# Prologue of a fused attention and maxout kernel: E and F turned together, keys of batch 0 projected four heads at once, fp32 filler

## The chip, the core and the metric

The kernel runs on one core of one Trainium2 chip. The metric is the device time of one execution in microseconds, the median of several runs. The profile shows one further execution; its span goes from the first to the last instruction, and its own time is a little longer than its span.

## What is computed

Linformer attention over 8 batches, 8 heads, 1024 positions and a head dimension of 64, followed by a maxout layer:

```python
k_proj = einsum('ks,bhsd->bhkd', E, k)            # E, F: 64 x 1024
v_proj = einsum('ks,bhsd->bhkd', F, v)
attn   = softmax(q @ k_proj^T / 8)                # over the 64 projected keys
x      = (attn @ v_proj), heads side by side      # 8192 x 512
h      = maximum(maximum(x @ w1, x @ w2), x @ w3) # 512 -> 768
out    = h @ w_out                                # 8192 x 512, float32
```

All inputs are float32 in memory. The kernel computes in bf16 with float32 accumulation.

## The kernel before

The work goes batch by batch, each batch in two halves of 512 positions. For every half the three maxout products (l1, L216), and the product with w_out (L240) fill TensorE; the attention of the next batch is put between them at slots written out by hand. The order of the instructions on every engine is the order of the program: the kernel has a manual schedule, and an engine that waits holds what stands behind it.

**The prologue** (L363 to L506) does batch 0 before that machinery runs, since nothing is loaded yet. It works on the first half of batch 0 (ch 0), with heads in pairs (groups g = 0 to 3; HEAD gives the order of heads 0, 1, 2, 3, 5, 4, 7, 6), while loads arrive.

*Loads.* SyncE and ScalarE issue E, F and the first half of q as float32 (L366 to L370). POOL issues all loads that change the type from float32 to bf16, in one queue: four of k (two heads each), three of v, the first of four parts of w1, the last of v, the other parts of w1, then w2, w3, the second half of q, w_out and the data of batch 1 (L378 to L393, L477 to L481). Eight of these may be under way; each later one waits for the one eight before it.

*E and F.* Each is held as 128 rows of 512 (two rows of the tile to a row of E), cast to bf16 (E on VectorE L401, F on ScalarE L402), and turned by multiplying with the identity, 16 matmuls of 64 columns each (L406), into one PSUM bank each. E is copied out on VectorE, F on ScalarE (L413). Before it copies F, ScalarE casts two pairs of q (L412). fT2 holds F twice side by side (L451), for wide value projections.

*Queries.* Cast by head (L423, L424), turned on TensorE in groups of two heads (q_turn0, L417), copied out on VectorE (L419).

*Keys.* k_proj0(g) (L275) projects one pair of heads: 16 matmuls with the keys as stationary operand, 64 columns each, which gives the projected keys already turned, heads on partitions. A cast (L280) puts them into kpT.

*Values.* v_proj0(g) (L282) does the same for the groups 0 and 1; v_wide0(g) (L289) does the groups 2 and 3 with the doubled F, 8 matmuls of 128 columns, and two copies.

*Scores and softmax.* scores0 (L298) and exp0 (L304) per group, into the banks SB = (0, 1, 4, 5). sums_part0(hh) (L312) sums over keys by multiplying with ones, for the head half hh (groups 0 and 1, or 2 and 3), and takes logarithm and inverse on ScalarE. kp_up0 (L325) spreads the projected keys by a selection matrix for the scores of the second half of the batch, used much later; VectorE copies them out (L330).

*Attention output and w1.* av0(f, hh) (L474) multiplies with the values; norm0 (L318) scales on VectorE and writes xT. w1_ct(ct) (L456) adds part ct of w1 for all six column tiles jt, each in its own bank W1B = (0, 1, 4, 5, 2, 3). The parts ct 0 and 1 need head half 0, the parts 2 and 3 head half 1. From w1_ct(1) on TensorE goes on with w2 and w3 (l1_first, L461).

The order on TensorE from the first half of the sums on is: the exponentials of all four groups are issued, sums_part0(0), v_proj0(0), kp_up0, sums_part0(1), fillers, v_proj0(1), a filler, av0 for head half 0, v_wide0(2), a filler, w1_ct(0), v_wide0(3), half of w1_ct(1), av0 for head half 1, and the rest of w1.

*Fillers.* warmup(n, bank) (L359) runs n matmuls of 512 columns on a tile of zeros whose result is not used. 24 of them stand in the prologue.

Of the kernel before, what the change touches and what calls it, by code (L numbers as in the profile page):

```python
# [9 lines left out]
FP32 = mybir.dt.float32  # L10
# [6 lines left out]
def kernel(ctx: ExitStack, tc: tile.TileContext, q, k, v, E, F, w1, w2, w3, w_out, out):  # L17
# [25 lines left out]
    eT = T([P, SI, KP], BF16, "eT")  # L43
    fT2 = T([P, SI, 2, KP], BF16, "fT2")
    fT = fT2[:, :, 0, :]
# [25 lines left out]
    ef_f = ef_b.bitcast(FP32).rearrange("p (x n) -> p x n", n=S // 2)  # L71
    ef_b = ef_b[:, 2 * S:3 * S].rearrange("p (x n) -> p x n", x=2)
# [45 lines left out]
    AB = 4  # L118
# [156 lines left out]
    def k_proj0(g):  # L275
        for si in range(SI):
            for u in range(2):
                nc.tensor.matmul(out=ps[u * D:(u + 1) * D, 2, g * KP:(g + 1) * KP], lhsT=k_t[0][:, HEAD[2 * g + u], si, :],
                                 rhs=eT[:, si, :], start=(si == 0), stop=(si == SI - 1))
        nc.vector.tensor_copy(out=kpT[0][:, g, 0, :], in_=ps[:, 2, g * KP:(g + 1) * KP])  # L280

    def v_proj0(g, bank):  # L282
        for si in range(SI):
            for u in range(2):
                nc.tensor.matmul(out=ps[half(g, u), bank, g * D:(g + 1) * D], lhsT=fT[:, si, :],
                                 rhs=v_t[0][:, HEAD[2 * g + u], si, :], start=(si == 0), stop=(si == SI - 1))
        nc.vector.tensor_copy(out=vp2[0][:, g], in_=ps[:, bank, g * D:(g + 1) * D].rearrange("p (dd f) -> p f dd", f=2))
# [10 lines left out]
    def scores0(ch, g, bank):  # L298
        for u in range(2):
            rows = slice(u * D, (u + 1) * D)  # L300
            nc.tensor.matmul(out=ps[half(g, u), bank, :], lhsT=kpT[0][rows, g, 0, :],
                             rhs=qT[0][rows, 4 * ch + g, :], start=True, stop=True)
# [9 lines left out]
    def sums_part0(hh):  # L312
        cols = slice(hh * 512, (hh + 1) * 512)
        quads0(0, 6, lambda rows, g: ones[rows, :], (hh,))
        nc.scalar.activation(out=lns[0][:, cols], in_=ps[:, 6 + hh, :], func=AF.Ln)
        nc.scalar.activation(out=rinv[0][:, cols], in_=lns[0][:, cols], func=AF.Exp, scale=-1.0)
# [8 lines left out]
    def kp_up0():  # L325
        for u in range(2):
            for f in range(2):
                nc.tensor.matmul(out=ps[:, u, f * 256:(f + 1) * 256], lhsT=sel[:, 2 * u + f, :],
                                 rhs=kpT[0][:, 0:NPAIR, 0, :], start=True, stop=True)
            nc.vector.tensor_copy(out=kp_0[:, u].rearrange("p f g k -> p (f g k)"), in_=ps[:, u, :])  # L330
# [7 lines left out]
    def scores_up0():  # L338
        for g in range(NPAIR):
            for f in range(2):  # L340
                for r in range(4):
                    rows = slice(r * HD, (r + 1) * HD)
                    for u in range(2):
                        nc.tensor.matmul(out=ps[half(g, u), AB + r, g * P:(g + 1) * P], lhsT=kp_0[rows, u, f, g, :],  # L344
                                         rhs=qT_1[rows, HEAD[2 * g + u]].rearrange("p (n f) -> p n f", f=2)[:, :, f],
                                         start=(f == 0), stop=(f == 1), tile_position=(r * HD, half(g, u).start))
# [15 lines left out]


    nc.scalar.preload_act_table_set("natural_log_exp_and_others")
    nc.vector.memset(warm, 0.0)
    nc.sync.dma_start(out=ef_f[:, 0], in_=E.rearrange("k (x n) -> (k x) n", x=2))  # L366
    nc.scalar.dma_start(out=ef_f[:, 1], in_=F.rearrange("k (x n) -> (k x) n", x=2))
# [32 lines left out]
    warmup(9, 7)  # L400
    nc.vector.tensor_copy(out=ef_b[:, 0], in_=ef_f[:, 0])  # L401
    nc.scalar.copy(out=ef_b[:, 1], in_=ef_f[:, 1])  # L402
    for y, dst in enumerate((eT, fT)):
        for si in range(SI):
            for x in range(2):
                nc.tensor.matmul(out=ps[x * D:(x + 1) * D, y, si * KP:(si + 1) * KP], lhsT=ef_b[:, y, si::SI],  # L406
                                 rhs=ident[:, x::2], start=True, stop=True)
        if not y:
            warmup(2, 3)
        if y:  # L410
            for g in (0, 1):
                nc.scalar.copy(out=q_0[:, :, 2 * g, :], in_=q_st[:, HEAD[2 * g]])  # L412
        (nc.scalar.copy if y else nc.vector.tensor_copy)(out=dst, in_=ps[:, y, :].rearrange("p (si k) -> p si k", k=KP))  # L413
# [7 lines left out]
    def q_cast0(g):  # L421
        if g > 1:
            nc.scalar.copy(out=q_0[:, :, 2 * g, :], in_=q_st[:, HEAD[2 * g]])  # L423
        nc.vector.tensor_copy(out=q_0[:, :, 2 * g + 1, :], in_=q_st[:, HEAD[2 * g + 1]])  # L424
# [7 lines left out]
    k_proj0(0)  # L432
    q_turn0(2)
    warmup(1, 3)
    k_proj0(1)
    scores0(0, 0, SB[0])
    exp0(0, 0, SB[0])
    q_turn0(3)
    warmup(1, 3)
    k_proj0(2)  # L440
    scores0(0, 1, SB[1])
    exp0(0, 1, SB[1])
    warmup(2, 3)
    k_proj0(3)
    scores0(0, 2, SB[2])
    exp0(0, 2, SB[2])
    warmup(1, 3)
    scores0(0, 3, SB[3])
    exp0(0, 3, SB[3])
    sums_part0(0)  # L450
    nc.vector.tensor_copy(out=fT2[:, :, 1, :], in_=fT)  # L451
# [30 lines left out]
    v_proj0(0, 3)  # L482
    kp_up0()
    sums_part0(1)
    warmup(3, 2)
    v_proj0(1, 3)
    warmup(1, 2)
# [4 lines left out]
    v_wide0(2, 3)  # L492
    warmup(1, 2)
# [145 lines left out]
```

## Time and profile before

| what | value |
|---|---|
| median of 3 runs | 395.08 us (394.8 to 395.1) |
| profiled execution, its own time | 394.77 us |
| its span | 392.9 us |
| granted TensorE clock, mean | 1.000 |
| instructions in the span | 6611 |
| first matmul of w1 (L458) | starts 18.26 us |
| first matmul of w2 and w3 (L467) | starts 25.03 us |
| first matmul of the steady stage (L216) | starts 42.83 us |

How to read the profile: PE is TensorE, PEld its weight loads, DVE VectorE, ACT ScalarE, POOL GpSimd, SP SyncE. Times are in microseconds from the first instruction of the span. In a timeline each row is a run of like instructions: start, length, engine, line, operation, out<-in, shape, count, and in brackets how long the engine had been idle ahead of it and what released it. In the chain that ended last each row is a start, a length and what the time went to. A few matmul records are missing from a trace, so counts can be a little low.

### The profile page before, as it was taken

What the parts mean: (1) busy time and instruction counts of PE and PEld (TensorE: products, weight loads), DVE (VectorE), ACT (ScalarE), POOL (GpSimd) and SP (SyncE); (2) the same over time, 40 slices, a digit from 0 to 9 for tenths busy, and PEclk for the clock granted to TensorE, in tenths of its full rate; (3) what the DMA queues carried; (4) which work ended last, traced back from release to release, by engine and by line L of the source; (5) the groups of instructions that cost most, each with busy time, mean ns of one, the idle gap of its engine ahead of it and who ended that gap; (6) DMA issues with size and microseconds to landing.
All of it is one profiled execution on the core that took longest, in us unless ns stands there. A gap on an engine that the chain in (4) does not pass through costs nothing.

```text
span 392.9 us, 6611 instructions
## 1 busy us (share of the span) xinstructions
PE 383.7 (98%) x2695; PEld 172.8 (44%) x2746; DVE 202.9 (52%) x305; ACT 162.2 (41%) x248; POOL 67.0 (17%) x110
## 2 busy tenths in 40 slices
PE   8999999999999999999999999999999999999996
PEld 4444444444444444444444444444444444444443
DVE  4447475755662566344753357524764446453341
ACT  4413448374326622454224732266134542222222
POOL 7452131072004300050000600000010000000000
PEclk9999999999999999999999999999999999999999
DMA  8999979799984994169511992131011111111022
GB/s 224 206 211 204 205 184 199 125 209 206 206 159 89 200 206 177 26 123 204 158 53 28 176 212 97 53 81 54 2 60 48 54 55 54 55 46 60 5 104 107
DMA packets 41309, 48.39 MB, mean 123 GB/s; under 512 B 9152, under 2 KB 36288, under 8 KB 41280
## 3 DMA queue, kind: packets, MB, share of 16 engines
q0 software_dynamic: 31792, 43.52, 54.1%
q1 hardware_dynamic: 8656, 3.54, 4.7%
q10 hardware_dynamic: 832, 0.92, 0.7%
q8 instruction: 21, 0.34, 0.3%
q14 instruction: 8, 0.07, 0.1%
HBM read 57.15 MB, written 16.78 MB: 188 GB/s over the span
## 4 chain that ended last, share of the span: by engine, by line
PE 93%; DMA 5%; issue 1%; ACT 1%; POOL 0%; POOLq 0%
PE ps L216 60%; PE ps L240 19%; PE ps L124 3%; PE ps L160 3%; DMA w_sb<-in_moe_w_dram 3%; PE ps L467 2%; PE ps L146 2%; DMA k_t<-in_k_dram 2%; PE ps L254 1%; PE ps L458 1%; ACT pT L348 1%; PE ps L272 0%; PE ps L233 0%; POOL k_t L376 0%; PE ps L344 0%
## 5 line engine op out<-in xcount | busy, mean ns | idle before, releaser
L216 PE MATMUL ps<-xT,w_sb 128*128 128x512 bf16 x1048 | 242.6, 379 | 1.7
L216 PEld LDWEIGHTS <-w_sb 128*128 128x128 bf16 x1080 | 103.7, 98 | 129.8 <-issue 8.0
L221 DVE TENSOR_TENSOR m<-ps,h1s 128x512 f32<-128x512 f32 x90 | 62.1, 690 | 131.1 <-PE ps L216 100.6
L240 PE MATMUL ps<-wo_sb,hT 128*128 128x512 bf16 x342 | 84.0, 379 | 0.4
L219 ACT COPY h1s<-ps 128x512 f32<-128x512 f32 x90 | 52.9, 588 | 72.7 <-PE ps L216 72.0
L242 ACT COPY o_acc<-ps 128x512 f32<-128x512 f32 x59 | 34.6, 586 | 100.6 <-PE ps L240 86.0
L223 DVE TENSOR_TENSOR hT<-ps,m 128x512 bf16<-128x512 f32 x90 | 62.0, 689 | 8.1
L247 POOL DMA_DIRECT2D out_dram<-o_acc x28 | 15.2, 542 | 252.4 <-ACT o_acc L242 245.9
L240 PEld LDWEIGHTS <-hT 128*128 128x128 bf16 x354 | 34.0, 98 | 42.2 <-issue 2.3
L180 DVE TENSOR_TENSOR xT<-ps,rinv 128x1024 bf16<-128x1024 f32 x28 | 33.4, 1218 | 11.3 <-PE ps L160 11.3
L151 ACT ACTIVATE pT<-ps 128x1024 bf16<-128x1024 f32 x28 | 27.1, 1020 | 4.8 <-PE ps L146 4.4
L106 DVE STREAM_TRANSPOSE qT<-q_t 128x512 f32<-128x512 f32 x28 | 18.5, 689 | 0.0
L90 POOL DMA_DIRECT2D v_t<-in_v_dram x21 | 15.3, 754 | 9.4 <-issue 3.5
L171 ACT ACTIVATE lns<-ps 128x1024 f32<-128x1024 f32 x14 | 13.6, 1023 | 3.9 <-PE ps L160 3.9
L174 ACT ACTIVATE rinv<-lns 128x1024 f32<-128x1024 f32 x14 | 14.8, 1061 | 0.0
L124 PE MATMUL ps<-k_t,eT 128*64 128x512 bf16 x56 | 13.4, 382 | 0.0
L126 PE MATMUL ps<-v_t,fT 128*64 128x512 bf16 x56 | 13.4, 382 | 0.0
L90 POOL DMA_DIRECT2D k_t<-in_k_dram x14 | 10.7, 776 | 5.6 <-DMA k_t<-in_k_dram 2.8
L130 ACT CAST kp<-ps 64x512 bf16<-64x512 f32 x7 | 4.0, 578 | 17.6 <-PE ps L126 17.6
L90 POOL DMA_DIRECT2D q_t<-in_q_dram x14 | 10.7, 779 | 1.5 <-DMA wo_sb<-in_moe_w_out_dram 1.1
L467 PE MATMUL ps<-xT,w_sb 128*128 128x512 bf16 x46 | 10.6, 379 | 0.2 <-issue 0.2
L132 DVE COPY kp<-kp 64x1536 bf16<-64x1536 bf16 x7 | 3.9, 552 | 12.7 <-ACT kp L130 12.7
(90 smaller groups left out, 163.1 us busy)
## 6 DMA issues: line engine op xcount, KB each, us to landing
out_dram<-o_acc POOLq DMA_DIRECT2D x30, 512.0 KB, 3.0
k_t<-in_k_dram POOLq DMA_DIRECT2D x14, 512.0 KB, 13.3
q_t<-in_q_dram POOLq DMA_DIRECT2D x14, 512.0 KB, 12.1
v_t<-in_v_dram POOLq DMA_DIRECT2D x18, 256.0 KB, 14.9
v_t<-in_v_dram POOLq DMA_DIRECT2D x7, 512.0 KB, 15.7
w_sb<-in_moe_w_dram POOLq DMA_DIRECT2D x4, 384.0 KB, 10.2
k_t<-in_k_dram POOLq DMA_DIRECT2D x4, 256.0 KB, 8.0
w_sb<-in_moe_w_dram POOLq DMA_DIRECT2D x4, 192.0 KB, 9.9
```

The source lines that it names most:

```text
L90: nc.gpsimd.dma_start(out=dst[b % NB][:, slots], in_=sv[:, heads])
L106: nc.vector.transpose(out=qT[b % NB][:, hs].bitcast(FP32).rearrange("p h n -> p (h n)"), in_=q_t[b % NB][:, hs].rearrange("p h si d -> p ( ...
L124: nc.tensor.matmul(out=ps[0:KP, bank, :], lhsT=eT[:, si, :], rhs=k_t[i][:, :, si, :], start=(si == 0), stop=(si == SI - 1))
L151: nc.scalar.activation(out=pT[i][:, 2 * u + gg].rearrange("p ch (t r n) -> p r (ch t) n", t=4, r=4), in_=ps[:, AB:AB + 4, gg * 256:(gg + 1 ...
L180: nc.vector.tensor_tensor(out=xT[b % 2][:, f::2, ch, :], in0=ps[:, bank:bank + 2, :], in1=rinv[ch].rearrange("p (u n) -> p u n", u=2), op= ...
L216: nc.tensor.matmul(out=ps[:, bank, :], lhsT=w_sb[i][:, ct, jt * P:(jt + 1) * P], rhs=xT[b % 2][:, ct, ch, :], start=(ct == 0), stop=(ct == ...
L219: nc.scalar.copy(out=h1s[jt % 2], in_=ps[:, bank, :])
L221: nc.vector.tensor_tensor(out=m12[jt % 2], in0=ps[:, bank, :], in1=h1s[jt % 2], op=ALU.max)
L223: nc.vector.tensor_tensor(out=hT[c % 2][:, jt, :], in0=ps[:, bank, :], in1=m12[jt % 2], op=ALU.max)
L240: nc.tensor.matmul(out=ps[:, bank, :], lhsT=hT[c % 2][:, jt, tt * P:(tt + 1) * P], rhs=wo_sb[:, jt, :], start=(jt == 0), stop=(jt == NJT - 1))
L242: nc.scalar.copy(out=o[:, tt, :], in_=ps[:, bank, :])
L467: nc.tensor.matmul(out=ps[:, bank, :], lhsT=w_sb[i][:, ct, jt * P:(jt + 1) * P], rhs=xT[0][:, ct, 0, :], start=(ct == 0), stop=(ct == NCT ...
```

## The change

It touches the prologue only; the later stage reads eT and fT from the new tile.

- E goes on partitions 0 to 63 and F on 64 to 127, one row each. Both casts work on both, split by columns: VectorE the first half, ScalarE the second. Eight matmuls of 128 columns turn E and F together, into two banks, which VectorE and ScalarE copy out. eT, fT and fT2 become views of one tile eff, with F copied a second time.
- ScalarE's two casts of q come behind its copy of E and F.
- The keys are projected four heads at once (k_nat0): E is the stationary operand, 8 matmuls of 256 columns; the result is copied to SBUF, turned by two matmuls (k_turn0) and copied to kpT. The heads of a group lie in their natural order, and scores0 and scores_up0 take them accordingly.
- All value groups use v_wide0, in the banks 0, 1, 5 and 7 (before: groups 0 and 1 with v_proj0 in bank 3, then 3 and 7).
- kp_up0 goes to the banks 2 and 3, and its copies to ScalarE (kp_out0). The first half of the sums comes ahead of the exponentials of groups 2 and 3, the inverse is a step of its own (sums_inv0), and kp_up0 and the second half of the sums come behind the value projection of group 1.
- Of the fillers, six are float32 of 256 columns (warmup4), four ahead of the turning of E and F and two behind; eleven stay in bf16.

```diff
-    eT = T([P, SI, KP], BF16, "eT")
-    fT2 = T([P, SI, 2, KP], BF16, "fT2")
-    fT = fT2[:, :, 0, :]
+    eff = T([P, SI, 3, KP], BF16, "eff")
+    eT, fT, fT2 = eff[:, :, 0, :], eff[:, :, 1, :], eff[:, :, 1:3, :]
...
-    def k_proj0(g):
+    kp_s = kp2[0].rearrange("k h f r dd -> k (h f r dd)")
+
+    def k_nat0(gg):
+        cols = slice(gg * 4 * D, (gg + 1) * 4 * D)
         for si in range(SI):
-            for u in range(2):
-                nc.tensor.matmul(out=ps[u * D:(u + 1) * D, 2, g * KP:(g + 1) * KP], lhsT=k_t[0][:, HEAD[2 * g + u], si, :],
-                                 rhs=eT[:, si, :], start=(si == 0), stop=(si == SI - 1))
-        nc.vector.tensor_copy(out=kpT[0][:, g, 0, :], in_=ps[:, 2, g * KP:(g + 1) * KP])
...
+            nc.tensor.matmul(out=ps[0:KP, 2, cols], lhsT=eT[:, si, :], rhs=k_t[0][:, 4 * gg:4 * gg + 4, si, :],
+                             start=(si == 0), stop=(si == SI - 1))
+        nc.vector.tensor_copy(out=kp_s[:, cols], in_=ps[0:KP, 2, cols])
+
+    def k_turn0(gg):
+        for g in (2 * gg, 2 * gg + 1):
+            nc.tensor.transpose(out=psb[:, 7, g * KP:(g + 1) * KP], in_=kp_s[:, g * P:(g + 1) * P],
+                                identity=ident[0:KP, 0:KP])
+        nc.vector.tensor_copy(out=kpT[0][:, 2 * gg:2 * gg + 2, 0, :],
+                              in_=psb[:, 7, gg * P:(gg + 1) * P].rearrange("p (g k) -> p g k", k=KP))
...
-    def sums_part0(hh):
+    def sums_part0(hh, bank):
         cols = slice(hh * 512, (hh + 1) * 512)
-        quads0(0, 6, lambda rows, g: ones[rows, :], (hh,))
-        nc.scalar.activation(out=lns[0][:, cols], in_=ps[:, 6 + hh, :], func=AF.Ln)
+        quads0(0, bank - hh, lambda rows, g: ones[rows, :], (hh,))
+        nc.scalar.activation(out=lns[0][:, cols], in_=ps[:, bank, :], func=AF.Ln)
+
+    def sums_inv0(hh):
+        cols = slice(hh * 512, (hh + 1) * 512)
         nc.scalar.activation(out=rinv[0][:, cols], in_=lns[0][:, cols], func=AF.Exp, scale=-1.0)
...
-            nc.vector.tensor_copy(out=kp_0[:, u].rearrange("p f g k -> p (f g k)"), in_=ps[:, u, :])
+
+    def kp_out0():
+        for u in range(2):
+            nc.scalar.copy(out=kp_0[:, u].rearrange("p f g k -> p (f g k)"), in_=ps[:, 2 + u, :])
...
+    warm4 = warm.bitcast(FP32)
+
+    def warmup4(n, bank):
+        for _ in range(n):
+            nc.tensor.matmul(out=ps[:, bank, 0:256], lhsT=warm4[:, 0:P], rhs=warm4, start=True, stop=True)
...
-    nc.sync.dma_start(out=ef_f[:, 0], in_=E.rearrange("k (x n) -> (k x) n", x=2))
-    nc.scalar.dma_start(out=ef_f[:, 1], in_=F.rearrange("k (x n) -> (k x) n", x=2))
+    nc.sync.dma_start(out=ef_f[0:KP], in_=E)
+    nc.scalar.dma_start(out=ef_f[KP:P], in_=F)
...
-    warmup(9, 7)
-    nc.vector.tensor_copy(out=ef_b[:, 0], in_=ef_f[:, 0])
-    nc.scalar.copy(out=ef_b[:, 1], in_=ef_f[:, 1])
-    for y, dst in enumerate((eT, fT)):
...
+    warmup4(4, 7)
+    warmup(1, 7)
+    nc.vector.tensor_copy(out=ef_b[:, 0:S // 2], in_=ef_f[:, 0:S // 2])
+    nc.scalar.copy(out=ef_b[:, S // 2:], in_=ef_f[:, S // 2:])
+    ef_ps = ps[:, 0:2, :].rearrange("p b (s k) -> p (b s) k", k=P)
+    for si in range(SI):
+        nc.tensor.matmul(out=ef_ps[:, si], lhsT=ef_b[:, si::SI], rhs=ident, start=True, stop=True)
+    nc.vector.tensor_copy(out=eff[:, 0:4, 0:2, :].rearrange("p s x k -> p s (x k)"), in_=ef_ps[:, 0:4])
+    nc.scalar.copy(out=eff[:, 4:8, 0:2, :].rearrange("p s x k -> p s (x k)"), in_=ef_ps[:, 4:8])
+    for g in (0, 1):
+        nc.scalar.copy(out=q_0[:, :, 2 * g, :], in_=q_st[:, 2 * g])
+    warmup4(2, 3)
...
     q_turn0(0)
     q_turn0(1)
     warmup(3, 3)
-    k_proj0(0)
     q_turn0(2)
...
+    q_turn0(3)
+    nc.vector.tensor_copy(out=eff[:, :, 2, :], in_=fT)
+    warmup(3, 3)
+    k_nat0(0)
+    warmup(2, 3)
+    k_turn0(0)
     warmup(1, 3)
...
+    for g in (0, 1):
+        scores0(0, g, SB[g])
+        exp0(0, g, SB[g])
     warmup(1, 3)
...
+    k_nat0(1)
+    sums_part0(0, 6)
+    sums_inv0(0)
+    k_turn0(1)
+    v_wide0(0, 0)
+    for g in (2, 3):
+        scores0(0, g, SB[g])
+        exp0(0, g, SB[g])
...
-    v_proj0(0, 3)
+    v_wide0(1, 1)
     kp_up0()
-    sums_part0(1)
-    warmup(3, 2)
-    v_proj0(1, 3)
-    warmup(1, 2)
+    sums_part0(1, 0)
+    kp_out0()
+    sums_inv0(1)
     av0(0, 0)
     av0(1, 0)
     norm0(0, 0, 6, (0,))
     norm0(0, 1, 7, (0,))
-    v_wide0(2, 3)
-    warmup(1, 2)
+    v_wide0(2, 5)
     w1_ct(0)
     v_wide0(3, 7)
     w1_ct(1, range(3))
```

## The prediction

> **What bounds the kernel now.** I read the chain that ended last first, then TensorE's timeline over the first 45 us, then the timelines of VectorE, ScalarE and POOL. The page: TensorE is busy nearly always, so only a shorter TensorE stream or a shorter wait can gain.
>
> ```profile
> span 392.9 us, 6611 instructions
> PE 383.7 (98%) x2695; PEld 172.8 (44%) x2746; DVE 202.9 (52%) x305; ACT 162.2 (41%) x248; POOL 67.0 (17%) x110
> PE 93%; DMA 5%; issue 1%; ACT 1%; POOL 0%; POOLq 0%
> ```
>
> The change lies wholly in the prologue. There the chain (start, length, what) is not TensorE at all:
>
> ```profile
> 1.47 0.84 POOL k_t L376
> 2.31 7.71 DMA k_t<-in_k_dram
> 10.02 0.29 issue
> 10.31 10.07 DMA w_sb<-in_moe_w_dram
> 20.38 0.27 issue
> 20.65 0.59 PE ps L458 x2
> ```
>
> Everything until 20.4 us is loads: POOL issues the second part of w1 at 10.31, when a key load frees its slot, it lands at 20.38, and w1_ct(1) waits for it. Three weight loads stand at 20.42 and two matmul records from 20.65, so the unrecorded first matmul began at about 20.43. TensorE's timeline of the stretch before (start, length, line):
>
> ```profile
> 14.63 0.61 PE L328 MATMUL ps<-kpT,sel 128*128 128x256 bf16 x4
> 15.17 0.40 PE L272 MATMUL ps<-pT,ones 64*32 64x512 bf16 x4
> 16.25 0.44 PE L285 MATMUL ps<-v_t,fT 128*64 128x64 bf16 x16
> 16.95 0.68 PE L272 MATMUL ps<-pT,vp 64*32 64x512 bf16 x8
> 17.55 0.62 PE L291 MATMUL ps<-v_t,fT 128*128 128x128 bf16 x8
> 18.26 1.46 PE L458 MATMUL ps<-xT,w_sb 128*128 128x512 bf16 x6
> 19.55 0.61 PE L291 MATMUL ps<-v_t,fT 128*128 128x128 bf16 x8
> 20.65 0.59 PE L458 MATMUL ps<-xT,w_sb 128*128 128x512 bf16 x2 [0.49 <-DMA w_sb<-in_moe_w_dram]
> ```
>
> The reader is to see two dates that TensorE doesn't set: 16.25, where the second value load lands, and 20.43. Between them it had only about 0.4 us to spare (19.55 plus 0.46 for eight wide value matmuls is 20.01). VectorE in that stretch:
>
> ```profile
> 17.52 1.29 DVE L320 TENSOR_TENSOR xT<-ps,rinv 128x512 bf16<-128x512 f32 x2 [0.56 <-PE ps L272]
> 18.72 0.45 DVE L295 CAST vp<-ps 64x64 bf16<-64x64 f32 x2
> ```
>
> After 20.43 I find no wait on a load in TensorE's rows up to 47 us (the waits view has one of 0.5 us, the one above), so a delay there is passed on to the end whole.
>
> **What the Trainium skill says.** "DMA: Bandwidth & Descriptors", section "Issuing engines are not separate DMA queues": loads from SP, ScalarE and POOL share the same 16 DMA engines. The trace agrees: in each 2 us stretch from 2 us on the DMA share is 0.98 or more, whoever issued. "TensorE: Matmul & The Clock Gate", Part 1: TensorE starts at half clock and is released after about 3.4 us of activity; a 512-column matmul takes 427 ns before, 216 after. The trace agrees: nine fillers take 3.68 us from 1.19, later 20 matmuls take 4.32 us (216 ns). "FP8 and Floating Point Precision", "TensorE Precision Notes": a true fp32 matmul makes four passes. No fp32 matmul is in this trace; estimate from that page: one fp32 filler of 256 columns costs two bf16 fillers of 512, 0.85 us cold, 0.43 warm. If it loads its weights four times in the open it is up to half longer, which I keep as the upper end.
>
> **The change, part by part.**
>
> *E and F turned together.* Before: 32 turns at 67 ns (16 from 4.81 to 5.88), 2.15 us, and two fillers. Now eight 128-column ones, 57 ns each (four query turns from 9.10 to 9.33) to 134 (twice the strided row): 0.5 to 1.1 us; I take 0.8. Both casts now wait for both loads (VectorE cast at 4.21, ScalarE at 4.46 before), so the turns start at about 4.46 + 0.62 = 5.1 instead of 4.81 and end at 5.9. Two copies of 0.6 to 0.7 follow, and ScalarE's two casts for groups 0 and 1 (0.85), before at 5.42 and ahead of its copy, now come behind it: query turns start at about 7.3, before 7.50. Query loads still admit the last group at 8.5. All this is covered by the wait for keys, which ended at 10.06. I cost it at 0; if fp32 fillers are half longer, about 1.3 us of cover is used up and some 0.3 us would show.
>
> *Keys four heads at once.* Before: 64 matmuls at 23 ns, 0.37 per pair, four casts. Now 16 of 256 columns at 107 ns (row L328: 0.43 for four), turns, four copies. The stream grows, 1.48 to 1.74 plus 0.25, but this stretch is a chain: landed 10.06; matmuls 0.87 and tail 0.25; copy of 256 columns 0.42 (between 0.22 for 64 and 0.69 for 512); turns and hand-over 0.4; copy 0.25; so scores at 12.25, exponentials at 12.7 (before 10.88), 1.25 for two, sums 0.45, logarithm 0.59, inverse 0.63, and only then the other two exponentials: 15.6 to 16.9. Before they ended at 14.64. Due next is the second half of the sums, at 17.15 by the next step, so 0.3 us is left: cost 0.
>
> *kp_up0 and the second half of the sums moved behind the second value load.* This is the step that costs. They ran at 14.63 and 15.17, in the wait for that load; now they queue behind it, with av0 behind them. Load ready about 16.15 (POOL saw it by 16.34, TensorE started at 16.25 behind fillers; range 16.1 to 16.25). Wide values 0.46 (17.55 to 18.01) → 16.61; kp_up0 0.54 (14.63 to 15.17) → 17.15; sums 0.33 → 17.48; av0 to the first normalisation 0.52 (21.18 to 21.70) → 18.00, against 17.52.
>
> *Bank of the third value group.* It goes from bank 3, which w1_ct(0) uses last, to bank 5, which it uses fourth. Its two copies (0.45) queue on VectorE behind both normalisations (1.29): 18.00 + 1.29 + 0.45 + 0.07 to hand over = 19.81. w1_ct(0) starts at 18.75, has done three by 19.40 and waits 0.4. The last three, 0.65 → 20.46; wide values of the last group 0.46 → 20.92 for w1_ct(1). kp_out0 on ScalarE ends at about 19.4 (logarithm to 18.2, two copies of 0.6), in time for jt 4 and 5; the inverse behind it at 20.05, needed at 22.2.
>
> *Loads.* POOL's order and waits are unchanged and the bytes are the same; E and F go as 4 KB rows on 64 partitions each: 0, between -0.1 and +0.1 us.
>
> Sum: 20.92 - 20.43 = +0.49 us. Against the profiled execution, span 392.9 and 394.77 in all, 395.26; that one lies 0.31 under the median of the runs, 395.08, so the forecast is 395.08 + 0.49 = **395.6**. About 0.2% (0.79 us) is what a measurement here tells from no change, so this counts as within it.
>
> **The rivals.**
> *Hidden (15%).* The wait for w1 stays last: the value load or the sums come 0.4 us earlier than I reckon, or the copies slip in ahead. Then 395.1. For it: TensorE's slack was 0.4; against: the two moved steps alone are 0.87.
> *Faster, TensorE's stream decides (4%).* Turns -1.35, keys +0.5, values +0.2 (32 at 23 ns to 16 at 57), fillers -0.2 (15 at 0.216 against ten and two fp32): -0.85, 394.2. Against: the chain shows loads, and their landing doesn't move.
> *Slower, the clock (15%).* fp32 fillers, or fewer fillers from 13 us on, leave TensorE at half clock when the key matmuls start at 10.06; from there it decides. The first eight then cost 0.87 more, of which 0.3 is slack: +0.57, 396.2. If half clock lasts to w1_ct(0), the 2.7 us from 16.15 to 20.92 grow by some 2 more: 398.2. I take 396.9. Against: bf16 fillers remain, and gaps are under 0.8 us.
> *Slower, the key chain (13%).* The exponentials come over 0.3 us later than 16.9, by late query turns or dearer copies, and hold the sums: 396.1.
> *My forecast (53%)* has its own range 395.2 to 395.9.
>
> **How the numbers follow.** Over 395.87: the clock 0.14, the key chain 0.10, the forecast's edge 0.08, 0.32. Under 394.29: 0.02 of the faster case. The rest, 0.66, is within 0.2%. The range leaves out the faster case and the worse half of the clock case: 394.9 to 396.9.
>
> **What would show it.** w1_ct(1) at about 20.9 without a wait on its load; first normalisation near 18.0; a wait on VectorE inside w1_ct(0); exponentials in pairs near 12.7 and 15.6; 512-column matmuls at 216 ns from 10 us on. A w1_ct(1) at 20.4 behind its load means the hidden case; matmuls at twice their length after 10 us mean the clock; a load that lands much earlier or later would upset everything here.

## The result, and the profile after

The changed kernel takes 396.40 us (median of 6 runs, 396.08 to 397.72), the kernel before 394.99 us (6 runs, 394.59 to 395.12). The ratio is 1.0042, 95% interval 1.0028 to 1.0056: slower by 1.4 us, or 0.36%. The forecast was 395.6, called no change. The time lies in the stated range of 394.9 to 396.9, but for another reason than the forecast gave, and beyond the 395.87 up to which the prediction spoke of no change; it gave a chance of 0.32 to a time over that.

The profiled execution of the changed kernel has an own time of 397.72 us with 3.1 us outside its span; in the other five that part is 1.8 to 1.9. So I compare spans: 394.6 against 392.9. From the page of the changed kernel:

```profile
span 394.6 us, 6447 instructions
PE 383.5 (97%) x2612; PEld 173.5 (44%) x2661; DVE 202.2 (51%) x305; ACT 163.0 (41%) x250; POOL 67.0 (17%) x110
PE 94%; DMA 2%; issue 1%; ACT 1%; DVE 0%; ACTq 0%; DVEq 0%
```

There are 164 instructions less (6611 before), and TensorE's busy time is the same within 0.2 us. The chain has moved from the loads of k and w1 to a load of q. Its first part (start, length, what):

```profile
2.23 8.49 DMA k_t<-in_q_dram
...
10.75 0.41 ACT q_t L435
...
11.21 0.40 PE ps L429 x4
11.61 0.65 PE ps L369 x3
12.26 0.99 PE ps L279 x8
...
19.39 0.68 DVE xT L325
20.06 0.53 issue
20.59 0.20 DVE vp L296
```

The last query load (its tile lies in k_t's buffer) lands at 10.7; then come its cast, its turns, three fillers (L369), and only then the projection of the first four heads of k. Before, the last cast of q was at 8.49, and the keys began when their own load came, at 10.06. TensorE's timeline of the changed kernel shows the same stretch as a chain of single steps:

```profile
11.21 0.40 PE L429 MATMUL ps<-ident,q_t 128*128 128x128 bf16 x4 [0.36 <-ACT q_t L435]
12.19 1.06 PE L279 MATMUL ps<-k_t,eff 128*64 128x256 bf16 x8
14.30 0.41 PE L303 MATMUL ps<-qT,kpT 64*64 64x512 bf16 x4
17.25 0.41 PE L303 MATMUL ps<-qT,kpT 64*64 64x512 bf16 x4
17.59 0.62 PE L292 MATMUL ps<-v_t,eff 128*128 128x128 bf16 x8
18.58 0.64 PE L271 MATMUL ps<-pT,ones 64*32 64x512 bf16 x4
20.22 1.67 PE L470 MATMUL ps<-xT,w_sb 128*128 128x512 bf16 x5 [0.22 <-DVE xT L325]
22.18 0.81 PE L470 MATMUL ps<-xT,w_sb 128*128 128x512 bf16 x3
```

The last row is w1_ct(1): 22.18, against 20.43 before, so 1.75 us later. w2 and w3 follow from 26.77 (before 25.03) and the steady stage from 44.57 (before 42.83): the same 1.74, and nothing of it is given back. It makes up the difference of the spans, 1.7. No wait on w1 stands at w1_ct(1) any more.

Why the query is late is read from the movement of data per microsecond. The windows view, first of the kernel before, then of the changed one (columns: window, its length in us, busy us and instructions of PE, PEld, DVE, ACT, POOL, then the TensorE clock, the DMA share and GB/s):

```profile
2.00:3.00 1.00, 1.00 (x4) 0.42 (x3) 0.00 (x0) 0.02 (x1) 1.00 (x2) 1.00 0.91 225
3.00:4.00 1.00, 1.00 (x4) 0.33 (x3) 0.00 (x0) 0.00 (x0) 1.00 (x3) 1.00 1.05 390
4.00:5.00 1.00, 1.00 (x7) 0.35 (x5) 0.52 (x1) 0.55 (x1) 1.00 (x2) 1.00 1.12 372
```

```profile
2.00:3.00 1.00, 1.00 (x3) 0.79 (x3) 0.00 (x0) 0.02 (x1) 1.00 (x2) 1.00 0.96 172
3.00:4.00 1.00, 1.00 (x4) 0.76 (x3) 0.00 (x0) 0.00 (x0) 1.00 (x3) 1.00 0.94 266
4.00:5.00 1.00, 1.00 (x4) 0.40 (x2) 0.00 (x0) 0.00 (x0) 1.00 (x2) 1.00 1.07 214
```

The DMA engines are as busy, and move 652 KB in place of 987 KB in these three microseconds. E and F lie ahead of q on both queues. By issue and time to landing, E lands at 4.77 and F at 5.87, before at 4.19 and 4.43. Each of the two casts now needs both loads, and they start at 5.97 and 5.95. The last query follows. In the kernel before (ScalarE's row, then VectorE's):

```profile
4.46 0.62 ACT L402 CAST v_t<-v_t 128x512 bf16<-128x512 f32 x1 [2.43 <-DMA v_t<-in_F_dram]
8.49 0.30 DVE L424 CAST q_t<-k_t 128x256 bf16<-128x256 f32 x1 [0.56 <-DMA k_t<-in_q_dram]
```

and in the changed kernel (ScalarE; its last cast of q is in the chain above):

```profile
5.95 0.62 ACT L417 CAST v_t<-v_t 128x512 bf16<-128x512 f32 x1 [3.93 <-DMA v_t<-in_F_dram]
```

In the packet records E's 64 packets of 4 KB take 305 ns and F's 258 ns, before 128 packets each of 2 KB 128 and 88 ns: 19.5 and 16.5 us of engine time for what cost 16.4 and 11.2. The prediction priced this at nothing.

The chain shows only what comes last. POOL's loads of k, which move at the same time, are late too. POOL issues the second part of w1 when the second load of k has landed (POOL's timeline, the kernel before, then the changed one):

```profile
10.31 0.56 POOL L384 DMA_DIRECT2D w_sb<-in_moe_w_dram  x1 [0.65 <-DMA k_t<-in_k_dram]
11.51 0.56 POOL L398 DMA_DIRECT2D w_sb<-in_moe_w_dram  x1 [1.03 <-DMA k_t<-in_k_dram]
```

That load lands at 11.22, before at 10.02. The first keys of the changed kernel need it, so even with early queries they could not start before about 11.25. Of the 2.13 us by which they start later (12.19 against 10.06), the late query and the fillers behind it account for the last 0.9 or so. The order of the program adds to this. Before, the keys of the first pair stood ahead of the turns of the last two query groups (8.72, against 9.10 and 10.77). In the changed kernel the keys of four heads stand behind all query turns and three fillers.

The Trainium skill has a statement on the loads of E and F, and I had not used it. "SBUF — State Buffer", section "Door 1: The DMA port swizzle", says that a transfer into partitions 0 to 63 reaches only half of the ports by which data enters SBUF, and the section "Can I just issue two DMAs to hit both halves?" that a second transfer into the other half, issued at the same time, does not make up for it. The change does just that: E into the lower half, F into the upper one. This trace agrees in the direction (266 against 390 GB/s in the fourth microsecond, 214 against 372 in the fifth); an experiment below tests the placement itself.

### The profile page after: what moved, and what is told of

Same layout as the page of the kernel before. It is cut to its first block, busy times and chain, and to the rows that moved or that the text cites. A ratio compares the mean times of both kernels' runs of the same rounds, so it can differ in the third digit from the quotient of the medians.

```text
span 394.6 us, 6447 instructions
## 1 busy us (share of the span) xinstructions
PE 383.5 (97%) x2612; PEld 173.5 (44%) x2661; DVE 202.2 (51%) x305; ACT 163.0 (41%) x250; POOL 67.0 (17%) x110
## 4 chain that ended last, share of the span: by engine, by line
PE 94%; DMA 2%; issue 1%; ACT 1%; DVE 0%; ACTq 0%; DVEq 0%
PE ps L215 59%; PE ps L239 19%; PE ps L123 3%; PE ps L159 3%; PE ps L479 2%; DMA k_t<-in_q_dram 2%; PE ps L145 2%; PE ps L470 1%; PE ps L253 1%; PE ps L271 1%; ACT pT L356 1%; PE ps L279 1%; PE ps L369 0%; PE ps L292 0%; PE ps L232 0%
## 5 line engine op out<-in xcount | busy, mean ns | idle before, releaser
L125 PE MATMUL ps<-v_t,eff 128*64 128x512 bf16 x56 | 13.4, 382 | 0.0
L123 PE MATMUL ps<-k_t,eff 128*64 128x512 bf16 x56 | 13.4, 382 | 0.0
L89 POOL DMA_DIRECT2D k_t<-in_k_dram x14 | 10.7, 776 | 6.2 <-DMA k_t<-in_k_dram 3.4
L89 POOL DMA_DIRECT2D q_t<-in_q_dram x14 | 10.7, 779 | 1.7 <-DMA wo_sb<-in_moe_w_out_dram 1.1
```

The costliest lines, as they stand in the source:

```text
L89: nc.gpsimd.dma_start(out=dst[b % NB][:, slots], in_=sv[:, heads])
L123: nc.tensor.matmul(out=ps[0:KP, bank, :], lhsT=eT[:, si, :], rhs=k_t[i][:, :, si, :], start=(si == 0), stop=(si == SI - 1))
```

## The experiments

My theory after the result: E and F in half the partitions each make the loads slow, the last query comes late, and the key chain, which has no slack, carries that to the end; the stall on the third value group's bank comes on top. Rivals: the size of the packets; the fp32 filler and the clock; the rest of the change (keys, sums, values). Each run stands beside runs of the kernel before on the same chip (medians 394.93, 394.98 and 394.96 us). Lines in diffs are against the changed kernel, but for two that start from the kernel before, and where another is named.

**1. E and F in pieces of 2 KB**, placed as in the changed kernel:

```diff
-    nc.sync.dma_start(out=ef_f[0:KP], in_=E)
-    nc.scalar.dma_start(out=ef_f[KP:P], in_=F)
+    nc.sync.dma_start(out=ef_f[0:KP], in_=E.rearrange("k (x n) -> k x n", x=2))
+    nc.scalar.dma_start(out=ef_f[KP:P], in_=F.rearrange("k (x n) -> k x n", x=2))
...
```

> The changed kernel, with one edit: E and F still go as one row per partition on 64 partitions each, but each row in two pieces of 2 KB into two separate places. In the profile of the changed kernel E landed at about 4.8 and F at 5.9 us (before: 4.2 and 4.5) and the last query load at 10.7 (before 8.5). Theory packets (rows of 4 KB are moved slowly and hold up what shares the DMA engines): E and F by 4.6, the last query load by 8.8, w1_ct(1) at 20.9 instead of 22.2, time 395.5. Theory half of the partitions (a load into 64 partitions is slow whatever its pieces): nothing changes, 396.4. Theory that the loads don't matter: 396.4 with loads landing early.

396.49 us, ratio 1.0051 (1.0038 to 1.0064). E and F are cast at 5.95 and 5.93, the last query at 10.66, w1_ct(1) starts at 22.10. All as in the changed kernel: the size of the packets is not the cause.

**2. The kernel before, with the E and F part of the change alone** (loads, casts, eight turns, two copies, bf16 filler; keys, sums and values as before):

```diff
-    nc.sync.dma_start(out=ef_f[:, 0], in_=E.rearrange("k (x n) -> (k x) n", x=2))
-    nc.scalar.dma_start(out=ef_f[:, 1], in_=F.rearrange("k (x n) -> (k x) n", x=2))
+    nc.sync.dma_start(out=ef_f[0:KP], in_=E)
+    nc.scalar.dma_start(out=ef_f[KP:P], in_=F)
...
-    for y, dst in enumerate((eT, fT)):
...
+    for si in range(SI):
+        nc.tensor.matmul(out=ef_ps[:, si], lhsT=ef_b[:, si::SI], rhs=ident, start=True, stop=True)
...
```

> The kernel before with only the E and F part of the change: loads on 64 partitions each, casts split by columns, eight turns, copies by halves, ScalarE's first two query casts behind its copy; fillers stay bf16, keys, values and order as before. Theory loads first: last query load near 10.7 and w1_ct(1) 0.5 to 1.2 us later than 20.4, 395.5 to 396.2. Theory order first (kp_up0 and sums behind the value load, bank 5): no change, 395.0.

395.87 us, 1.0024 (1.0015 to 1.0034): this part alone costs 0.9 us. The last two queries are cast at 10.21, w1_ct(1) starts at 21.49. In its timeline of TensorE:

```profile
9.24 0.44 PE L277 MATMUL ps<-eff,k_t 128*64 128x64 bf16 x16
10.67 0.40 PE L413 MATMUL ps<-ident,q_t 128*128 128x128 bf16 x4 [0.98 <-ACT q_t L419]
11.56 0.44 PE L277 MATMUL ps<-eff,k_t 128*64 128x64 bf16 x16 [0.50 <-DVE kpT L279]
```

The keys of the first pair are projected at 9.24, without any wait for E: the cover of that wait was real. What holds TensorE here is the late query behind them. But it is not the only late date: the second load of k landed at 10.68 (before 10.02), and the second part of w1 at 21.30 (before 20.38), 0.19 us ahead of w1_ct(1). With early queries this execution would have waited for w1 instead, so its 0.9 us can't be put down to the queries alone.

**3. The changed kernel with the E and F part of the kernel before**, fp32 filler as changed. The inverse of the diff above, with this filler:

```diff
+        if not y:
+            warmup4(1, 3)
...
-    warmup4(2, 3)
+    warmup4(1, 3)
```

> The changed kernel with the E and F part of before: 128 rows of 2 KB each, 32 turns, E copied on VectorE and F on ScalarE, ScalarE's first two query casts ahead of its copy; the fp32 fillers stay. Theory loads first: 395.5, and what is left over the kernel before is the order of the sums and bank 5, with first normalisation near 18.0 and w1_ct(1) near 20.9. Theory order first: 396.4.

Of 13 executions ten lie at 394.82 to 395.35, three at 398.36 to 398.44 with a span of 396.5. Median 395.22, 1.0024 (1.0004 to 1.0043); most of that ratio is the three. In the profiled one the last two queries are cast from 8.51 on, the keys start at 10.56, and w1_ct(1) at 20.56, 0.13 later than before.

**4. Filler in bf16 throughout**, the rest as changed:

```diff
-    warmup4(4, 7)
-    warmup(1, 7)
+    warmup(9, 7)
...
-    warmup4(2, 3)
+    warmup(4, 3)
```

> The changed kernel with its six fp32 fillers put back as bf16 ones (nine ahead of the turns, four behind). Theory clock: query and key work runs faster, 395.5 or less. Theory loads and theory order: no change, 396.4 within 0.2.

396.69 us, 1.0048 (1.0033 to 1.0063); its span 394.2 to 394.7, the changed kernel's 394.3 to 394.7. By chance this profile shows what half clock does, in TensorE's timeline:

```profile
6.39 1.07 PE L419 MATMUL ps<-ident,v_t 128*128 128x128 bf16 x8 [1.17 <-ACT v_t L416]
7.26 1.91 PE L369 MATMUL ps<-warm 128*128 128x512 bf16 x4
8.96 1.06 PE L428 MATMUL ps<-ident,q_t 128*128 128x128 bf16 x8
```

Eight turns of E and F take 1.07 us in place of the changed kernel's 0.71, and four fillers start 425 ns apart on average (7.26 to 8.96), where 512-column matmuls later take 216. It ends before the keys at 12.08; the turn of the last query waits for its cast anyway, and w1_ct(1) starts at 22.08. So neither fp32 filler nor a clock that is late by some microseconds is the cause.

**5. E on the even, F on the odd partitions**, so that each load covers the whole range; the copies out of PSUM take the columns apart again:

```diff
-    nc.sync.dma_start(out=ef_f[0:KP], in_=E)
-    nc.scalar.dma_start(out=ef_f[KP:P], in_=F)
+    nc.sync.dma_start(out=ef_f[0:P:2], in_=E)
+    nc.scalar.dma_start(out=ef_f[1:P:2], in_=F)
...
```

> The changed kernel with E on the even partitions and F on the odd ones, still one row of 4 KB per partition and 64 rows per load; the copies out of PSUM take the columns apart again. Cutting the rows in 2 KB pieces had changed nothing. Theory half of the partitions (a load that writes only partitions 0 to 63 or 64 to 127 is slow because of where it writes): E and F land by 4.6 instead of 4.8 and 5.9, the last query load by 8.8, time 395.2 to 395.5. Theory rows (64 rows are slow wherever they go): 396.4 as the changed kernel.

Of six executions three have a span of 393.7 or 393.8, against the changed kernel's 394.3 to 394.7, the others 394.2, 395.5 and 396.4. The median, 397.45, 1.0056 (1.0036 to 1.0077), doesn't tell of the prologue: four executions spend 2.3 to 3.9 us outside their span. The timeline of ScalarE in the profiled one (span 393.8):

```profile
4.69 0.62 ACT L417 CAST v_t<-v_t 128x512 bf16<-128x512 f32 x1 [2.67 <-DMA v_t<-in_F_dram]
...
9.36 0.41 ACT L435 CAST q_t<-k_t 128x256 bf16<-128x256 f32 x1 [2.05 <-DMA k_t<-in_q_dram]
10.01 0.40 ACT L435 CAST q_t<-k_t 128x256 bf16<-128x256 f32 x1 [0.24 <-DMA k_t<-in_q_dram]
```

F is cast 1.26 us earlier (5.95 in the changed kernel): with the placement alone changed, E and F land at 3.80 and 4.61, as early as before or nearly. The rate comes back as well. In the fifth microsecond all six profiles with E and F in halves (the changed kernel, 1, 2, 4, 6 and 7) move 192 to 215 GB/s; this one and number 9, the two with alternating partitions, move 372 and 374, and the kernels with the old loads 372 to 384. This bears out the skill's statement on halves.

But the last query, forecast to land by 8.8, lands at 9.98 and is cast at 10.01, still 1.5 us behind the kernel before. Its gain of 0.74 us on the changed kernel is in good part spread: with the same loads as the changed kernel, numbers 6 and 7 cast it at 10.29 and 10.38, and number 9, with the loads of this one, at 10.38. So the placement explains the slow loads of E and F. That it makes the queries late is not shown.

**6. The bank of the third value group last**: w1_ct(0) takes bank 5 as its sixth, not as its fourth.

```diff
-    W1B = (0, 1, 4, 5, 2, 3)
+    W1B = (0, 1, 4, 2, 3, 5)
```

> The changed kernel, but w1_ct takes its banks in the order 0, 1, 4, 2, 3, 5, so that the bank of the third value group comes last again. Theory of the prediction (the bank's two copies behind both normalisations hold w1_ct(0)): the wait inside w1_ct(0) goes, w1_ct(1) starts 0.3 to 0.45 us earlier than 22.2, time 396.0. Rival (what follows waits for something else that is just as late): 396.4.

395.95 us, 1.0025 (1.0016 to 1.0035). TensorE's timeline:

```profile
19.76 1.46 PE L470 MATMUL ps<-xT,w_sb 128*128 128x512 bf16 x6 [0.22 <-DVE xT L325]
21.05 0.61 PE L292 MATMUL ps<-v_t,eff 128*128 128x128 bf16 x8
21.50 0.81 PE L470 MATMUL ps<-xT,w_sb 128*128 128x512 bf16 x3
```

From w1_ct(0) to w1_ct(1) it takes 1.74 us, in the changed kernel 1.96: the stall is real and costs 0.22, not the 0.4 that I forecast. w1_ct(1) starts 0.68 earlier than in the changed kernel; the other 0.46 is that in this profile the last query was cast at 10.29 instead of 10.75, with the same loads. The medians differ by 0.45.

**7. Without the three fillers ahead of the first keys**:

```diff
     nc.vector.tensor_copy(out=eff[:, :, 2, :], in_=fT)
-    warmup(3, 3)
     k_nat0(0)
```

> The changed kernel without the three fillers between the last query turn and the first key matmuls. In the changed kernel the last query turn starts at 11.2, the keys have landed, and the fillers run from 11.44 to 12.19 ahead of the key matmuls. Theory query loads (the chain last query load, turn, keys, scores is what is late): key matmuls start 0.65 us earlier, time 395.75. Rival (something later holds the chain, or the clock falls without them): 396.4 or more.

397.02 us, 1.0052 (1.0037 to 1.0066); four spans of six are 394.2 to 394.4, two 395.8 and 396.5. The forecast of 395.75 missed. The keys start at 11.16 and w1_ct(0) at 19.20, both 1.0 earlier (0.37 of it because the last query was cast at 10.38), and then:

```profile
21.82 0.82 PE L469 MATMUL ps<-xT,w_sb 128*128 128x512 bf16 x3 [0.50 <-DMA w_sb<-in_moe_w_dram]
```

A load of w1 takes the place of the chain. It came at about 21.8, later than the 20.4 of the kernel before; a packet of 16 KB of the queue that the profile calls instruction, 19.72 to about 20.7, lies in the same stretch. The earlier start of 1.0 us left 0.36 at w1_ct(1).

**8. Keys, sums and values of the change, with the old E and F part and bf16 filler**: as number 3, and:

```diff
-    warmup4(4, 7)
-    warmup(1, 7)
+    warmup(9, 7)
...
-            warmup4(1, 3)
+            warmup(2, 3)
...
-    warmup4(1, 3)
+    warmup(2, 3)
```

> The changed kernel with the E and F part of before and bf16 fillers in place of the fp32 ones (nine, two, two). The same kernel with fp32 fillers gave 395.2, but 3 of its 13 executions lay at 398.4 with a span longer by 3.4 us. Theory fp32 filler (it doesn't always release the clock in time): 395.2 with no execution over 396. Rival (the key stage or the lower count of fillers later on lets the clock fall now and then): still some near 398.4.

394.96 us in 13 runs (394.8 to 395.27), 1.0000 (0.9993 to 1.0008). TensorE's timeline:

```profile
10.22 1.06 PE L279 MATMUL ps<-k_t,eff 128*64 128x256 bf16 x8
15.63 0.62 PE L292 MATMUL ps<-v_t,eff 128*128 128x128 bf16 x8
18.34 1.59 PE L473 MATMUL ps<-xT,w_sb 128*128 128x512 bf16 x6 [0.30 <-DMA w_sb<-in_moe_w_dram]
20.34 0.82 PE L473 MATMUL ps<-xT,w_sb 128*128 128x512 bf16 x3
```

Both parts of w1 wait for their loads again. With early loads and bf16 filler, the rest of the change costs nothing that shows. The part with E and F costs 396.40 - 394.96 = 1.44 us on top of it; the fp32 filler, which differs too, had no effect in number 4.

**9. All that the runs so far charge, taken out of the changed kernel**: E and F on even and odd partitions (as 5), bank 5 last (6), no filler ahead of the keys (7), bf16 filler (4). The four diffs together, the core of them:

```diff
-    nc.sync.dma_start(out=ef_f[0:KP], in_=E)
+    nc.sync.dma_start(out=ef_f[0:P:2], in_=E)
...
-    warmup(3, 3)
     k_nat0(0)
...
-    W1B = (0, 1, 4, 5, 2, 3)
+    W1B = (0, 1, 4, 2, 3, 5)
```

> The changed kernel with the three parts that the runs so far charge taken out together: E on the even and F on the odd partitions, the third value group's bank taken last by w1_ct(0), no filler ahead of the keys' turns, and bf16 filler. If these are all the causes, w1_ct(1) begins at about 20.4 (21.44 with the loads alone, less 0.45 for the bank, less about 0.6 for the filler), the span is 392.9 to 393.1 and the time 394.8 to 395.0, as before. Rival: the late last query (10.0 with these loads) still binds; then w1_ct(1) is at 20.9 or later and the time 395.3 or more.

395.59 us in 21 runs (395.11 to 398.37), 1.0025 (1.0015 to 1.0035): the first theory falls short, and the rival is right. In the profiled run (395.2, span 393.4) E and F are cast at 4.63 and 4.62, but the last query at 10.38, later still than in number 5; the keys start at 11.17 and w1_ct(1) at 20.95.

**10. The same, with the first two loads of q ahead of E and F**, their casts and turns first too:

```diff
-    nc.sync.dma_start(out=ef_f[0:KP], in_=E)
-    nc.scalar.dma_start(out=ef_f[KP:P], in_=F)
...
         (nc.scalar if g % 2 else nc.sync).dma_start(out=q_st[:, 2 * g:2 * g + 2], in_=qv_[0][:, 2 * g:2 * g + 2])
+        if g < 2:
+            (nc.scalar if g else nc.sync).dma_start(out=ef_f[g:P:2], in_=F if g else E)
...
```

> As the spread kernel, but the first two query loads are issued ahead of E and F, and their casts and turns come first. If it is what is queued ahead of them that makes the queries late, the first two are cast at about 4 to 5 and the last at 8.5 to 9.5, E and F at 5.5 to 6.5, and the time is at most 395.0. Rival: the total of the loads sets the date of the last of them, whichever it is; then E and F come at 8 or later, the keys wait for them, and the time is 395.4 or more.

396.45 us in 5 runs (395.6 to 396.79), 1.0039 (1.0026 to 1.0052), three of them with 2.3 to 3.2 us outside the span, the other two with spans of 394.7 and 395.0. In the profiled run, the shortest of the five (span 393.1), the first two queries are cast at 4.4, F at 6.09, the last query still at 9.86 (ScalarE's timeline):

```profile
4.40 0.76 ACT L428 CAST q_t<-k_t 128x256 bf16<-128x256 f32 x2 [2.37 <-DMA k_t<-in_q_dram]
6.09 0.62 ACT L434 CAST v_t<-v_t 128x512 bf16<-128x512 f32 x1 [0.94 <-DMA v_t<-in_F_dram]
...
9.86 0.40 ACT L423 CAST q_t<-k_t 128x256 bf16<-128x256 f32 x1 [0.48 <-DMA k_t<-in_q_dram]
```

The first theory had 8.5 to 9.5 for the last query and missed; the rival had E and F at 8 or later, and they came at about 6. What comes last on these queues comes late here too. w1_ct(1) starts at 20.43, the date of the kernel before, with no gain over it.

**11. The kernel before with fp32 filler**:

```diff
-    warmup(9, 7)
+    warmup4(4, 7)
+    warmup(1, 7)
...
-            warmup(2, 3)
+            warmup4(1, 3)
```

> The kernel before with fp32 filler alone: 4 and 1 in place of 9 bf16 ones, 1 in place of 2. Typical time as before, 394.9 to 395.1, if the filler is off the path. If fp32 filler is what left a longer span in three of thirteen executions of the changed kernel with the old E and F, some executions are near 398; with none among the executions, that stays open.

395.06 us in 14 runs, 1.0004 (0.9996 to 1.0012). Two of the 14 lie at 396.0 and 396.3 (spans 394.1 and 394.4), none near 398. So whether fp32 filler made the three long executions of number 3 stays open.

**12. Number 8 with bank 5 last and without the filler ahead of the keys**, the fastest version that these findings suggest. Against number 8:

```diff
-    warmup(3, 3)
     k_nat0(0)
...
-    W1B = (0, 1, 4, 5, 2, 3)
+    W1B = (0, 1, 4, 2, 3, 5)
```

> The changed kernel with E and F as before, bf16 filler, the third value group's bank taken last and no filler ahead of the keys' turns. If w1_ct(0) and w1_ct(1) are held by the loads of w1 once the keys are early, the time is 394.7 to 395.0, no better than before. Rival: TensorE's stream sets the end, and the time is 394.0 to 394.4.

395.00 us in 13 runs (394.71 to 395.53), 1.0004 (0.9996 to 1.0012). The keys start at 9.92, and w1_ct(0) then waits 0.55 us for its load, at 18.29, and w1_ct(1) 0.20, at 20.40. No version here beats the kernel before. In this one and in number 8 its bound stands: the loads of w1 as POOL's queue delivers them.

**What the profiles say together.** For each profile of the changed order: the start of the first keys (k), the start of w1_ct(1) (w), and the span.

| kernel | last cast of q | k | w | w - k | span |
|---|---|---|---|---|---|
| changed | 10.75 | 12.19 | 22.18 | 9.99 | 394.6 |
| 1, pieces of 2 KB | 10.66 | 12.10 | 22.10 | 10.00 | 394.6 |
| 4, bf16 filler | 10.7 | 12.08 | 22.08 | 10.00 | 394.5 |
| 5, even and odd | 10.01 | 11.44 | 21.44 | 10.00 | 393.8 |
| 3, old E and F | 8.9 | 10.56 | 20.56 | 10.00 | 393.0 |
| 6, bank last | 10.29 | 11.72 | 21.50 | 9.78 | 393.9 |
| 9, even and odd, bank last | 10.38 | 11.17 | 20.95 | 9.78 | 393.4 |
| 10, query first, bank last | 9.87 | 10.65 | 20.43 | 9.78 | 393.1 |
| 7, no filler | 10.38 | 11.16 | 21.82 | 10.66 (load) | 394.2 |
| 8, old E and F, bf16 | 8.79 | 10.22 | 20.34 | 10.12 (load) | 392.9 |
| 12, as 8, tuned | 8.7 | 9.92 | 20.40 | 10.48 (load) | 392.8 |

(10.7, 8.9 and 8.7 are the second of two casts in one row, about 0.35 us after its start.) From the first keys to w1_ct(1) the prologue is a rigid chain of 9.78 us, plus 0.22 where the bank stalls; or it waits for w1, at 20.3 to 20.4. From w1_ct(1) to the end of the span it takes 372.4 to 372.7 in every row, and 372.5 in the kernel before. So the time is read from two dates: k plus 9.78, and the landing of w1. The kernel before and numbers 8 and 12 lie on the second; number 7 too, where its load was late; the rest lie on the first.

The second date is not fixed. From the second load of k on, POOL's loads land one behind the other at steady steps. The second part of w1 lands 9.6 us after that load of k in seven of the fourteen profiles. In the other seven it takes 10.2 to 11.0, because one load of the row lands about 1 us behind its step; each time this comes after the start of a packet of 16 KB of the instruction queue (13.70 in the kernel before). In the changed kernel that packet starts at 20.72, too late for this part of w1. So although its load of k is 1.20 us late, this part lands only 0.43 later, at 20.81 against 20.38. Even with early keys, these loads would not have let the changed kernel start w1_ct(1) before about 20.8. In number 10 this part landed at 19.68, and there the chain from the keys holds.

**What stays open.** Why the last loads of q are late even with E and F spread. The packet records show where: KB moved per microsecond by each queue.

| | | 4 to 5 | 5 to 6 | 6 to 7 | 7 to 8 | 8 to 9 us |
|---|---|---|---|---|---|---|
| before | SP | 174 | 184 | 67 | 2 | 0 |
| | ScalarE | 190 | 107 | 127 | 80 | 6 |
| | POOL | 0 | 8 | 81 | 148 | 193 |
| 5, even and odd | SP | 233 | 14 | 109 | 99 | 34 |
| | ScalarE | 150 | 142 | 14 | 97 | 108 |
| | POOL | 0 | 94 | 124 | 82 | 107 |

Where the second load of a queue ends, the third now starts late: 0.81 us on SP's queue from 4.89 on, 1.01 on ScalarE's from 5.58, before at most 0.21. Number 10 has 0.92 and 1.44 there, and with the halves there are such gaps too (0.96 and 1.00 in number 6). Meanwhile POOL's key loads come in, and the third loads must share with them. The gap goes with the new form of the loads (all kernels with the old form pass from load to load in under 0.1 us, or 0.21 in the kernel before), but no view shows what fills it. SP and ScalarE also took 0.56 us to issue a load of E or F in place of 0.40. What was not tried is a load of E and F on 64 partitions behind all of q.

Nor was the plainest rival tried: the keys put back ahead of the turns of the last two query groups, which the first scores don't need. In the profile of the changed kernel they could then have started when their load was there, at about 11.25 instead of 12.19, and in that of number 10 at about 10.1 instead of 10.65. These are estimates from the landing dates 11.22 and 10.07. They say that up to 0.9 us of the loss may be a matter of order, and not of the loads.

Also open: the time outside the span. It is 1.7 to 2.0 us in all executions of the kernel before and of numbers 2, 3, 6, 8, 11 and 12, and 2.3 to 3.9 in some of the changed kernel (1 of 6), of 1, 4, 5, 7, 9 and 10. All of these have the new loads, but so have numbers 2 and 6, which never show it.

## Why the prediction was off where it was

*E and F turned together, cost 0.* The working was right where it looked: the turns took 0.71 us (forecast 0.8), and the copies and casts hide behind the wait for the last query. It took E and F as landed by 4.46. F landed at 5.87, and query turns that were to begin at about 7.3 began at 8.32. That all this was "covered by the wait for keys" was too kind as well. In the new order the turns of the last query and three fillers stand ahead of the keys: from its cast to the keys it takes 1.44 us (10.75 to 12.19). A cast at the expected 8.5 leaves about 0.1 us before the 10.06 of the keys, so hardly any lateness of the query was covered.

*Loads, "0, between -0.1 and +0.1 us".* **This step failed.** "The bytes are the same" was taken to mean the same landing. Runs 2, 3 and 8 show that the E and F part, with what hangs on it, is the whole of the loss: 0.9 us in the kernel before, 1.44 in the changed one. That it is the loads is read from the landings: E, F, the queries and the keys all land late. Run 5 shows that the placement in half the partitions slows E and F, and that spreading them doesn't bring the last query back; run 1 shows that the size of the packets has no share. Why the queries stay late is open. "Query loads still admit the last group at 8.5" was the sentence that broke: it was cast at 10.75. The "landed 10.06" of the keys broke with it: their second load landed at 11.22.

*Keys four heads at once, cost 0 with 0.3 us of slack.* The chain itself was worked out well. From the start of the keys I had 2.19 us to the scores, 2.64 to the first exponentials, 5.54 to the second ones; measured 2.11, 2.56 and 5.50 (scores 14.30, exponentials at 14.75 and 17.69). Only its start moved, by 2.13 us, from 10.06 to 12.19. I wrote "the exponentials come over 0.3 us later than 16.9, by late query turns or dearer copies", gave it 13%, and in the main that rival is what happened: the exponentials ended at 18.77. Its 396.1 was 0.3 too low, since the queries, and the keys, were later than I allowed.

*kp_up0 and the sums behind the second value load, first normalisation at 18.00.* In run 8, where the start is as I assumed, it stands at:

```profile
17.42 1.29 DVE L325 TENSOR_TENSOR xT<-ps,rinv 128x512 bf16<-128x512 f32 x2 [0.59 <-PE ps L271]
```

That is 0.58 early, and 0.10 before the 17.52 of the kernel before. The failing term is "load ready about 16.15": in run 8 the value projection starts at 15.63, right behind the scores, without a wait. In the kernel before, that load lands at 16.06, 2.26 us behind the load ahead of it, in run 8 at 15.21, 1.26 behind; the former trace has a packet of 16 KB of the instruction queue at 13.70, 0.89 us long, which run 8 has at 16.16. So I had built on a date that such a packet seems to have delayed, and on a TensorE start that came behind filler. In run 8 the moved steps cost nothing, since w1's load comes last; where the keys are late they are part of the 9.78 us.

*Bank of the third value group, a wait of 0.4.* The wait is there: VectorE's copies come behind both normalisations, as forecast, but the three matmuls ahead of the wait start later against them than I took. In the changed kernel (VectorE's timeline):

```profile
19.39 1.29 DVE L325 TENSOR_TENSOR xT<-ps,rinv 128x512 bf16<-128x512 f32 x2 [0.59 <-PE ps L271]
20.59 0.45 DVE L296 CAST vp<-ps 64x64 bf16<-64x64 f32 x2
```

w1_ct(0) starts 0.83 us after the first normalisation (I had 0.75), and the wait costs 0.22. With early keys w1's load hides it (run 8).

*The sum.* Forecast 20.92 for w1_ct(1), measured 22.18. The difference, 1.26, is the keys' start, +2.13; the value load that no longer holds the chain, -0.74 (7.20 us from keys to normalisation, forecast 7.94); and -0.13 from there to w1_ct(1) (2.79, forecast 2.92). The forecast of 395.6 was only 0.8 off because an error of 2.1 us was in part cancelled by another. That is luck; its +0.49 is no confirmation of its mechanism.

*The clock.* 512-column matmuls take 216 ns from 11 us on, as forecast. One fp32 filler costs about two bf16 ones, as estimated: four and one bf16 take 4.06 us at the start of the changed kernel, nine bf16 ones 3.68 in the kernel before and 4.02 in run 12. The rival is not shown, but for the rare long executions that stay open. (Its "2.7 us from 16.15 to 20.92" is no length: that stretch is 4.77 us long.)

## What to carry to other kernels

Price a reshaped load by the partitions it fills and by what is queued behind it, not by its bytes: here, in the six profiles with E and F on 64 partitions each, F landed 0.8 to 1.4 us later than before, the last query 1.8 to 2.3, and the second load of k, on another queue, 0.6 to 1.2. Before calling a chain free, write down the slack of its first date and look at every load that can move that date. And check that a date taken from a trace is not itself delayed by something that comes and goes, such as a packet of the instruction queue.

## What the runs showed of the hardware

- Two loads of 64 rows each into the two halves of the partitions: 192 to 215 GB/s in the fifth microsecond (six profiles); on alternating partitions 372 and 374 (runs 5 and 9).
- Packets of 4 KB of these loads: F's 238 to 276 ns in halves, 174 and 172 alternating. E's overlap: 203 to 305 in halves, 214 and 252 alternating.
- After such loads, in either placement, the next load but one on the same queue starts late: 0.8 to 1.4 us in runs 5 and 10, 0.96 and 1.00 in run 6; at most 0.21 with the old loads. The cause is unknown.
- A packet of 16 KB of the instruction queue takes 0.9 us. It came at 13.7 us in the kernel before and at 16 to 21 us in those of the changed order. In the profiles of the kernel before, of run 7 and of run 8 one of POOL's loads then under way landed about 1 us behind its usual step (2.26 after the load ahead of it in place of 1.3; 2.44 and 1.76 in place of 0.9 to 1.0). In run 7 TensorE waited 0.50 us for it.
- TensorE at half clock from 6.4 to about 10 us (run 4) did not make w1_ct(1) later: 22.08, against 22.18.
